# A fused attention and swish product: two more batches on tiles of the array, and an output block that opens the output product with one wait

## Chip, cores, metric

One core of one Trainium2 chip. The metric is the device time of the kernel in microseconds (us), median of several runs, with a granted TensorE clock of 0.996 to 1.0. A profiled run also has a span, which leaves out the start and the end (271.7 of 273.8 us before). Engines: PE is TensorE's matmul, DVE VectorE, ACT ScalarE, POOL GpSimd, SP SyncE.

## The reference

```python
# q, k, v: (8 batches, 8 heads, 576, 64)
q_s = softmax(q, over its 64 features);  k_s = softmax(k, over the 576 positions)
kv = einsum('bhsd,bhse->bhde', k_s, v)             # 64 x 64 a head
x  = einsum('bhsd,bhde->bhse', q_s, kv)            # to 4608 tokens x 512
h  = x @ w_in                                      # 512 -> 2048
out = (h * sigmoid(beta * h)) @ w_out              # 2048 -> 512, float32
```

## The kernel before

It works in nine slabs, t = 0 to 8: the first 512 rows of batch t, and in slab 8 the last 64 rows ("remainders") of all batches. Pass 1 of a slab computes h in 16 tiles of four 512-column matmuls; ACT empties each bank through Silu. Pass 2 is the product with w_out, from slab 1 on in a form with 7/8 of the multiplications: 112 matmuls of 256 columns on sums and differences of blocks, which DVE makes. The attention of batch t+1 is woven in (softmax, keys times values, and the outputs, which are queries times that result): `todo` holds (tick, step) pairs, a slab has 64 ticks in pass 1 and 64 in pass 2 (a product is 32/56 of a tick).

`add` records an instruction with what it reads (`r`), writes (`w`) and which PSUM banks it touches (`bank`). Waits on semaphores are derived from these; an engine that already knows of a count does not wait for it again. The eight banks are shared out:

```python
HB = (0, 1, 2)   # pass 1 tiles, in rotation; one of them takes the first product sum of pass 2
OB = (3, 4)      # the other two product sums, z5 and z2
MB = (5, 6, 7)   # attention
```

Words used below: a *block* is the output matmuls of one batch (QT with KVD), with or without remainders; a *half block* is half of them. A *key burst* is all the keys-times-values matmuls of one batch (VB with EK, and EKR for the remainder) in one go. The *transposed queries* (QT) come by a DMA transposition from slab 1 on. A *difference* is DVE's subtraction GT<-GT; the last 32 products of a pass 2 need two of them. The *entry* is what a change into tiles adds between two starts of PE. The *head* of a pass is its first few matmuls.

Batches 4 to 7 use tiles of the array: two 64-column tiles for keys times values, four 64 x 64 tiles for the output. Batches 0 to 3 multiply with full 128 x 128 matrices, one half of which is masked to zero.

```python
def tiled(b): return b > 3

def quad(b, pi=None):                   # outputs of batch b, and remainders of the pair pi
    bks = list(MB) + [HB[(hrot[0] + 1) % 3], HB[(hrot[0] + 2) % 3]]
    b_r = bks[4]                        # one bank for the remainders of both row halves
    ...                                 # x_mm, r_mm: matmuls with tile_position=(64 * a, 64 * c)
    x_mm(0, 1); r_mm(0); x_mm(0, 0); x_mm(1, 1); x_mm(1, 0); r_mm(1)
    # r_mm(1) waits on a semaphore until r_mm(0) has left the bank
    ...                                 # 4 copies to SBUF by DVE and ACT, 1 by DVE for the remainders

def attn(b):                            # slabs 4 to 6; ticks from the start of the slab
    return [(24 if b == 5 else 16, steps(kv_all, b)),
            (90, one(quad, b, b - 4 if b > 5 else None))]

def pass2_fast(t, tick, hooks):
    s, z5, z2 = HB[hrot[0] % 3], OB[0], OB[1]
    ...
    at(0)                               # ACT: exponentials of batch t + 2
    prod_s(range(0, 6)); prod(z5, ..., range(0, 6)); ...
```

The softmax here doesn't subtract the row's maximum and nothing guards it: scores larger than these inputs give would overflow.

Of the kernel before, what the change touches and what calls it, by code (L numbers as in the profile page):

```python
# [158 lines left out]
def bass_efficient_attn_shen__then__act_swish_beta_kernel(  # L159
# [12 lines left out]
    with ExitStack() as es:  # L172
# [130 lines left out]


        def tiled(b):
            return b > 3

        def pair(b, hp):
            if tiled(b):
# [133 lines left out]
        def kd(b):  # L443
            return b if b < 2 else 2 + b % 4
# [60 lines left out]
        def out_step(b, hp, pool=MB, eng=DVE):  # L505
            i = b % 2

            def one():
                bk = bank(pool)
                out_mm(b, hp, bk)  # L510
                add(eng, lambda e: (e.copy if eng == ACTE else e.tensor_copy)(  # L511
                    XT[i][:, hp, :], PS[bk][:, :]),
                    r=[("ps", bk)], w=[("xt", i, hp)], bank=[bk])
            return [one]

        def outr_steps(b):
            pi = b // 2
            st = {}

            def one(hp, e_):  # L520
                if hp == 0 and e_ == 0:
                    st["b"] = bank()
                bk = st["b"]
                c = hp * 128 + e_ * 64
                d = kd(2 * pi + e_)
                mm(PS[bk][:, c:c + 64], KVD[d][:, hp, :], QTR[:, hp, 64 * e_:64 * e_ + 64],
                   True, True, r=[("kvd", d, hp), "qtr"], w=[("ps", bk)], bk=bk)
                if hp == 3 and e_ == 1:
                    o = bass.AP(XT8, pi * 128, [[NM * SM, 128], [SM, NM], [1, 128]])
                    add(DVE, lambda e: e.tensor_copy(o, PS[bk][:, :]), r=[("ps", bk)],  # L530
                        w=[("xt8", pi)], bank=[bk])
            return [lambda hp=hp, e_=e_: one(hp, e_) for hp in range(NHP) for e_ in range(2)]

        def quad(b, pi=None):
            i = b % 2
            bks = list(MB) + [HB[(hrot[0] + 1) % 3], HB[(hrot[0] + 2) % 3]]
            b_r = bks[4]

            def x_mm(g, a):
                rows = slice(64 * a, 64 * a + 64)  # L540
                for c in range(2):
                    hp, bk = 2 * g + c, bks[2 * g + a]
                    add(PE, lambda e, c=c, hp=hp, bk=bk: e.matmul(  # L543
                        PS[bk][64 * c:64 * c + 64, :], KVD[kd(b)][rows, hp, 0:D],
                        QT[i][rows, hp, :], start=True, stop=True,
                        tile_position=(64 * a, 64 * c), skip_group_check=True),
                        r=[("kvd", kd(b), hp), ("qt", i, hp)], w=[("ps", bk)], bank=[bk])

            def r_mm(a):
                rows = slice(64 * a, 64 * a + 64)  # L550
                for g, e_, c in ([(g, e_, c) for g in range(2) for e_ in range(2)
                                  for c in range(2)] if pi is not None else ()):
                    hp, d, o = 2 * g + c, kd(2 * pi + e_), 256 * a + 128 * g + 64 * e_
                    op = add(PE, lambda e, c=c, hp=hp, d=d, o=o, e_=e_: e.matmul(
                        PS[b_r][64 * c:64 * c + 64, o:o + 64], KVD[d][rows, hp, 0:D],
                        QTR[rows, hp, 64 * e_:64 * e_ + 64], start=True, stop=True,
                        tile_position=(64 * a, 64 * c), skip_group_check=True),
                        r=[("kvd", d, hp), "qtr"], w=[("ps", b_r)], bank=[b_r])
                    if not done or done[0][0] == a:
                        done[:] = done[-1:] + [(a, op)]  # L560
                    else:
                        op.hard = [o_ for a_, o_ in done if a_ != a]

            done = []
            x_mm(0, 1)
            r_mm(0)
            x_mm(0, 0)
            x_mm(1, 1)
            x_mm(1, 0)
            r_mm(1)  # L570
            for x in (1, 0, 3, 2):
                eng, bk = (DVE, ACTE)[x % 2], bks[x]
                add(eng, lambda e, eng=eng, x=x, bk=bk: (  # L573
                    e.copy if eng == ACTE else e.tensor_copy)(XT[i][:, x, :], PS[bk][:, :]),
                    r=[("ps", bk)], w=[("xt", i, x)], bank=[bk])
            if pi is not None:
                o = bass.AP(XT8, pi * 128, [[NM * SM, 128], [SM, 2], [2 * SM, 2], [1, 128]])
                a = bass.AP(PS[b_r], 0, [[512, 128], [256, 2], [128, 2], [1, 128]])
                add(DVE, lambda e: e.tensor_copy(o, a), r=[("ps", b_r)], w=[("xt8", pi)],  # L579
                    bank=[b_r])  # L580

        def turn(b, hp0, n):
            i = b % 2
# [19 lines left out]
        def one(fn, *a):  # L603
            return lambda: fn(*a)

        def steps(fn, *a):
            return lambda: go(fn(*a))
# [2 lines left out]
            return kv_steps(b, (0, 1)) + kv_steps(b, (2, 3))  # L610

        def attn(b):
            return [(24 if b == 5 else 16, steps(kv_all, b)),
                    (90, one(quad, b, b - 4 if b > 5 else None))]

        def attn_late(b):
            if b < 4:
                x = []
                for hp in range(2):
                    x += out_step(b, hp, MB, ACTE if hp % 2 else DVE)  # L620
                s = spread(kv_steps(b, (0, 1)), 97, 101) + spread(kv_steps(b, (2, 3)), 101, 105)
                s += [(105, lambda: g_diff(1))]
                return s + spread(x, 117, 120)
            s = [(96, steps(kv_all, b)), (99, lambda: g_diff(1))]
            return s + [(112, one(quad, b))]

        def spread(steps, lo, hi):
            return [(lo + (hi - lo) * k / len(steps), s) for k, s in enumerate(steps)]
# [94 lines left out]

        def pass1_mm(t, f, m, bk):
            x = XT8 if t == 8 else XT[t % 2]
            rd = [("xt8", p_) for p_ in range(4)] if t == 8 else [("xt", t % 2, m)]
            mm(PS[bk][:, :], WIN[:, m, 128 * f:128 * f + 128], x[:, m, :], m == 0,
               m == NM - 1, r=rd + [("win", f, m)], w=[("ps", bk)], bk=bk)
            if m == NM - 1:
                add(ACTE, lambda e: e.activation(GT[:, f, :], PS[bk][:, :], ACT.Silu,  # L730
                                                 scale=BETA[:, f:f + 1]),
                    r=[("ps", bk), "beta"], w=[("gt", f, 0), ("gt", f, 1)], bank=[bk])
# [86 lines left out]
        def pass2_fast(t, tick, hooks):  # L819
# [66 lines left out]
            def at(n):  # L886
                for f in hooks.get(n, ()):
                    f()

            at(0)  # L890
            def prod_s(part):
                prod(s, lambda i, u: GS1[:, i, 128 * u:128 * u + 128], lambda i: [("gs1", i)],
# [46 lines left out]
        for t in range(NSLAB):  # L939
            todo = []  # L940
            if t == 0:
                todo = [(x, steps(t_steps, 1, (hp,), NOW, ACTE))
                        for hp, x in enumerate((97, 106, 114, 119))]
                todo += [(107, one(exp_kr_s, 1))]
                todo += [(x, one(exp_k, 1, hp, 1)) for hp, x in enumerate((108, 115, 120, 125.5))]
                todo += [(x, one(cast_v, 1, hp, DVE))
                         for hp, x in ((1, 118.5), (2, 123), (3, 127))]
                todo += [(x, steps(kv_steps, 1, (hp,), NOW))
                         for hp, x in enumerate((118, 122, 126))]
                todo += [(x, steps(out_step, 1, hp, NOW, ACTE)) for hp, x in enumerate((122.5, 125))]  # L950
                todo += [(117, one(o2_evac, 0, 0, 3, ACTE))]
                todo += [(2, steps(out_step, 0, 3, HEAD, DVE))]
            elif t < 4:
                todo = attn_late(t + 1)
                if t > 1:
                    todo += [(1, steps(out_step, t, 2, MB, ACTE)), (2.5, steps(out_step, t, 3))]
                if t == 3:
                    todo += [(4, one(norm_turn, 4, 2))]
                if t == 1:
                    todo += [(1, steps(out_step, 1, 2, (3,), ACTE)),  # L960
                             (3, steps(kv_steps, 1, (3,), (7,))),
                             (6, steps(out_step, 1, 3, (7,), DVE)),
                             (6.1, one(w_sum, 2, 4, 4)), (6.2, one(w_diff, 0)),
                             (6.3, one(w_diff, 1))]
            elif t < 7:
                todo = attn(t + 1)
                if t == 4:
                    todo += spread(outr_steps(3), 72, 88)
            elif t == 7:
                todo = spread(outr_steps(1), 32, 48)  # L970
            todo = sorted(todo, key=lambda x: -x[0])
# [151 lines left out]
```

## Time and profile before

| | before |
|---|---|
| time, median of the first 3 runs | 273.82 us |
| span of the profiled run | 271.7 us |
| PE / DVE / ACT busy | 97% / 71% / 67% |
| a slab without attention in pass 2 | 12.23 us of pass 2 |

The prediction tells how a stretch of the profile is read. In the trace of before some matmul records are missing (PE has 1918 beside 1937 weight loads); where I compare stretches, an end is put one matmul earlier if its own record is missing.

### The profile page before, as it was taken

What the parts mean: (1) busy time and instruction counts of PE and PEld (TensorE: products, weight loads), DVE (VectorE), ACT (ScalarE), POOL (GpSimd) and SP (SyncE); (2) the same over time, 40 slices, a digit from 0 to 9 for tenths busy, and PEclk for the clock granted to TensorE, in tenths of its full rate; (3) what the DMA queues carried; (4) which work ended last, traced back from release to release, by engine and by line L of the source; (5) the groups of instructions that cost most, each with busy time, mean ns of one, the idle gap of its engine ahead of it and who ended that gap; (6) DMA issues with size and microseconds to landing.
All of it is one profiled execution on the core that took longest, in us unless ns stands there. A gap on an engine that the chain in (4) does not pass through costs nothing.

```text
span 271.7 us, 4870 instructions
## 1 busy us (share of the span) xinstructions
PE 264.3 (97%) x1918; PEld 164.7 (61%) x1937; DVE 192.4 (71%) x408; ACT 181.1 (67%) x286; POOL 62.1 (23%) x80
## 2 busy tenths in 40 slices
PE   8999999999999999999999999999999999999994
PEld 2544454448844885477547864677457745874683
DVE  4964586887867799869776976678686649625762
ACT  4998658789287957897778847883783387018610
POOL 2790010006530099001900570126000100000000
PEclk9999999999999999999999999999999999999999
DMA  7999999989799139920499999112600030012005
GB/s 214 321 204 207 227 326 349 291 231 367 175 340 271 78 62 298 339 80 2 97 315 262 315 330 200 74 29 50 214 0 2 19 157 0 0 60 96 0 3 154
DMA packets 59366, 45.93 MB, mean 169 GB/s; under 512 B 28608, under 2 KB 58320, under 8 KB 58320
## 3 DMA queue, kind: packets, MB, share of 16 engines
q1 hardware_dynamic: 54480, 40.90, 53.0%
q0 software_dynamic: 4240, 4.19, 9.3%
q10 hardware_dynamic: 624, 0.53, 0.6%
q8 instruction: 15, 0.25, 0.4%
q14 instruction: 7, 0.06, 0.1%
HBM read 36.71 MB, written 9.44 MB: 170 GB/s over the span
## 4 chain that ended last, share of the span: by engine, by line
PE 88%; DVE 5%; DMA 2%; SPq 2%; issue 1%; ACT 0%
PE PS L406 51%; PE PS L830 35%; DMA VF<-in_v_dram 2%; PE PS L482 1%; PE PS L543 1%; DVE QS L357 1%; SPq L278 1%; SPq L290 1%; DVE EQ L361 1%; DVE XT L573 1%; DVE VB L377 1%; DVE TS L908 0%; DVE XT L579 0%; DVE QI L359 0%; DVE XT L511 0%
## 5 line engine op out<-in xcount | busy, mean ns | idle before, releaser
L406 PE MATMUL PS<-XT,WIN 128*128 128x512 bf16 x562 | 126.0, 379 | 1.1 <-issue 0.3
L730 ACT ACTIVATE GT<-PS,BETA 128x512 bf16<-128x512 f32 x144 | 95.2, 690 | 37.7 <-PE PS L406 37.4
L406 PEld LDWEIGHTS PS<-XT,WIN 128*128 128x128 bf16 x576 | 55.3, 98 | 64.6 <-DVE XT L511 0.6
L753 DVE TENSOR_SCALAR GT<-GT,RB 128x512 bf16<-128x512 bf16 x144 | 53.3, 392 | 36.3 <-ACT GT L730 35.5
L361 POOL TENSOR_TENSOR EQ<-EQ,QI 128x1024 bf16<-128x1024 bf16 (+1 forms) x13 | 25.6, 1967 | 50.6 <-DVE QI L359 50.0
L830 PE MATMUL PS<-WOUT,GT 128*128 128x256 bf16 x256 | 32.2, 273 | 0.4 <-DVE TS L908 0.4
L830 PE MATMUL PS<-WOUT,GS 128*128 128x256 bf16 x256 | 31.3, 273 | 0.0
L830 PE MATMUL PS<-WSUM,GT 128*128 128x256 bf16 x256 | 30.1, 273 | 0.3 <-DMA QT<-EQ 0.2
L830 PEld LDWEIGHTS PS<-WSUM,GT 128*128 128x128 bf16 x256 | 24.8, 98 | 3.9 <-issue 0.9
L830 PEld LDWEIGHTS PS<-WOUT,GT 128*128 128x128 bf16 x256 | 24.7, 98 | 3.6 <-DVE TS L908 0.9
L866 ACT COPY O2S<-PS 128x512 f32<-128x512 f32 (+1 forms) x17 | 9.4, 561 | 26.2 <-PE PS L830 25.0
L830 PEld LDWEIGHTS PS<-WOUT,GS 128*128 128x128 bf16 x256 | 24.3, 98 | 3.3 <-issue 0.4
L319 ACT ACTIVATE EQ<-QF 128x512 bf16<-128x512 f32 x32 | 18.0, 621 | 7.6 <-DMA QF<-in_q_dram 7.5
L789 DVE TENSOR_TENSOR GS<-GT 128x512 bf16<-128x512 bf16 (+2 forms) x32 | 21.9, 685 | 0.0
L357 DVE TENSOR_REDUCE QS<-EQ 128x16 f32<-128x1024 bf16 (+1 forms) x20 | 19.7, 985 | 0.8 <-ACT EQ L319 0.8
L796 DVE TENSOR_TENSOR GT<-GT 128x2048 bf16<-128x2048 bf16 x16 | 19.8, 1262 | 0.0
L377 POOL CAST VB<-VF 128x512 bf16<-128x512 f32 x24 | 14.8, 616 | 21.9 <-DVE GS L789 13.2
L319 ACT ACTIVATE EK<-KF 128x512 bf16<-128x512 f32 x32 | 18.1, 621 | 0.1
L878 DVE TENSOR_TENSOR O2S<-TS,PS 128x512 f32<-128x512 f32 (+1 forms) x17 | 10.7, 643 | 8.7 <-PE PS L830 8.7
L830 PE MATMUL PS<-WSUM,GS 128*128 128x256 bf16 x128 | 16.6, 273 | 0.0
L406 PE MATMUL PS<-WOUT,GT 128*128 128x512 bf16 x62 | 15.0, 379 | 0.1
L784 DVE TENSOR_TENSOR GS<-GT 128x256 bf16<-128x256 bf16 (+2 forms) x32 | 13.6, 426 | 1.1
(90 smaller groups left out, 215.8 us busy)
## 6 DMA issues: line engine op xcount, KB each, us to landing
out_dram<-O2S SPq DMA_DIRECT2D x8, 1024.0 KB, 5.0
QF<-in_q_dram SPq DMA_DIRECT2D x6, 1024.0 KB, 6.3
KF<-in_k_dram SPq DMA_DIRECT2D x6, 1024.0 KB, 8.7
VF<-in_v_dram SPq DMA_DIRECT2D x6, 1024.0 KB, 12.1
KF<-in_k_dram SPq DMA_DIRECT2D x8, 256.0 KB, 5.6
VF<-in_v_dram SPq DMA_DIRECT2D x8, 256.0 KB, 5.6
WOUT<-in_moe_w_out_dram POOLq DMA_DIRECT2D x4, 512.0 KB, 16.4
WIN<-in_moe_w_in_dram POOLq DMA_DIRECT2D x3, 512.0 KB, 9.2
```

The source lines that it names most:

```text
L319: add(ACTE, lambda e, o=o, a=a: e.activation(o, a, ACT.Exp), r=[(name + "f", i, hp)], w=[("e" + name, i, hp)])
L357: add(DVE, lambda e: e.tensor_reduce(s_, a, AX.X, ALU.add), r=ks, w=[("qs", i, hp0)])
L361: add(eng, lambda e: e.tensor_tensor(a, a, vb, ALU.mult), r=ks + [("qi", i, hp0)], w=ks)
L377: add(eng, lambda e: (e.copy if eng == ACTE else e.tensor_copy)(o, a), r=[("vf", i, hp), ("vone", i)], w=[("vb", i, hp)], after=after)
L406: add(PE, lambda e: e.matmul(o, l, r_, start=start, stop=stop), r=r, w=w, bank=[bk])
L730: add(ACTE, lambda e: e.activation(GT[:, f, :], PS[bk][:, :], ACT.Silu, scale=BETA[:, f:f + 1]), r=[("ps", bk), "beta"], w=[("gt", f, 0), ...
L753: add(DVE, lambda e: e.tensor_scalar(GT[:, f, :], GT[:, f, :], RB[:, f:f + 1], None, ALU.mult), r=k + ["rb"], w=k)
L784: add(DVE, lambda e: e.tensor_tensor(GS1[:, i:i + n, :], gv(i, 0, n), gv(i + NG, 1, n), ALU.add), r=gk(i, 0, n) + gk(i + NG, 1, n), w=[("g ...
L789: add(DVE, lambda e: e.tensor_tensor(GS2[:, i:i + n, :], GT[:, i:i + n, :], GT[:, i + NG:i + NG + n, :], ALU.add), r=[k_ for f in (i, i + ...
L796: add(DVE, lambda e: e.tensor_tensor(gv(f, th, NG), gv(f, th, NG), gv(f, 1 - th, NG), ALU.subtract), r=gk(f, 0, NG) + gk(f, 1, NG), w=gk(f ...
L830: add(PE, lambda e, l=l, r_=r_, st=st, u=u, i=i, b_=b_: e.matmul(PS[b_][:, 256 * u:256 * u + 256], l, r_, start=st, stop=end and i == NG - ...
L878: add(DVE, lambda e, b_=b_, u0=u0, u1=u1: e.tensor_tensor(o[:, u0:u1, :], ts[:, u0:u1, :], bank3(b_)[:, u0:u1, :], ALU.add), r=["ts", ("ps ...
```

## The change

The intent: tiles for batches 2 and 3 too, so that half of a full matmul is not spent on zeros; one wait for the whole block instead of waits inside it; two banks for the remainders, so that the two row halves run at once; and the block at the head of pass 2, so that its copies fall where DVE is idle.

```diff
-            return b > 3
+            return b > 1
@@ quad
-            bks = list(MB) + [HB[(hrot[0] + 1) % 3], HB[(hrot[0] + 2) % 3]]
-            b_r = bks[4]
+            if len(gs) == 1:
+                bks = [bank(), bank()]
+            else:
+                bks = list(MB) + [HB[(hrot[0] + 1) % 3], HB[(hrot[0] + 2) % 3], OB[1]]
+            b_r = bks[4:6]
+            first = [dict(r=..., bank=used)]        # the first tile waits for all keys and all banks
...
-            x_mm(0, 1); r_mm(0); x_mm(0, 0); x_mm(1, 1); x_mm(1, 0); r_mm(1)
+            r_mm(1); x_mm(0, 0); x_mm(0, 1); x_mm(1, 0); x_mm(1, 1); r_mm(0)
@@ attn
-            return [(24 if b == 5 else 16, steps(kv_all, b)),
-                    (90, one(quad, b, b - 4 if b > 5 else None))]
+            return [(24 if b == 5 else 16, steps(kv_all, b))]
@@ attn_late, batches 2 and 3 (slabs 1 and 2)
-            ... keys spread over ticks 97 to 105, outputs at 117 and 118.5, a DVE difference at 105
+            return [(97, steps(kv_all, b)), (97.01, lambda: g_diff(1)), (118, one(quad, b, (0,)))]
@@ pass2_fast
+            if 3 < t < 7:
+                quad(t + 1, (0, 1), t - 3)
             at(0)
@@ head of pass 1, slabs 2 and 3
-                    todo += [(1, steps(out_step, t, 2, MB, ACTE)), (2.5, steps(out_step, t, 3))]
+                    todo += [(1.5, one(quad, t, (1,)))]
@@ slab 4
-                    todo += spread(outr_steps(3), 72, 88)     # remainders of batches 2 and 3
```

(The diff is cut; statements of one kind are joined in a line.)

More of the change, by code (lines that the diff above doesn't have):

```diff
@@ L530, in one, with quad, tile @@
                     add(DVE, lambda e: e.tensor_copy(o, PS[bk][:, :]), r=[("ps", bk)],
-                        w=[("xt8", pi)], bank=[bk])
+                        w=[("xt8", pi, 0), ("xt8", pi, 1)], bank=[bk])
             return [lambda hp=hp, e_=e_: one(hp, e_) for hp in range(NHP) for e_ in range(2)]
-        def quad(b, pi=None):
+        def quad(b, gs=(0, 1), pi=None):
             i = b % 2
-            bks = list(MB) + [HB[(hrot[0] + 1) % 3], HB[(hrot[0] + 2) % 3]]
-            b_r = bks[4]
+            if len(gs) == 1:
+                bks = [bank(), bank()]
+            else:
+                bks = list(MB) + [HB[(hrot[0] + 1) % 3], HB[(hrot[0] + 2) % 3], OB[1]]
+            b_x = {2 * g + a: bks[2 * n + a] for n, g in enumerate(gs) for a in range(2)}
+            b_r = bks[4:6]
+            rem = pi is not None
+            used = list(b_x.values()) + (b_r if rem else [])
+            first = [dict(
+                r=[k_ for g in gs for c in range(2)
+                   for k_ in (("kvd", kd(b), 2 * g + c), ("qt", i, 2 * g + c))]
+                + ([("kvd", kd(2 * pi + e_), hp) for e_ in range(2) for hp in range(NHP)]
+                   + ["qtr"] if rem else []), bank=used)]
+            def tile(o, l, r_, a, c, bk, keys):
+                kw = dict(r=keys, bank=[bk])
+                if first:
+                    kw = first.pop()
+                add(PE, lambda e: e.matmul(o, l, r_, start=True, stop=True,
+                                           tile_position=(64 * a, 64 * c), skip_group_check=True),
+                    w=[("ps", bk)], **kw)
             def x_mm(g, a):
@@ L541, in x_mm @@
                 for c in range(2):
-                    hp, bk = 2 * g + c, bks[2 * g + a]
-                    add(PE, lambda e, c=c, hp=hp, bk=bk: e.matmul(
-                        PS[bk][64 * c:64 * c + 64, :], KVD[kd(b)][rows, hp, 0:D],
-                        QT[i][rows, hp, :], start=True, stop=True,
-                        tile_position=(64 * a, 64 * c), skip_group_check=True),
-                        r=[("kvd", kd(b), hp), ("qt", i, hp)], w=[("ps", bk)], bank=[bk])
-            def r_mm(a):
-                rows = slice(64 * a, 64 * a + 64)
-                for g, e_, c in ([(g, e_, c) for g in range(2) for e_ in range(2)
-                                  for c in range(2)] if pi is not None else ()):
-                    hp, d, o = 2 * g + c, kd(2 * pi + e_), 256 * a + 128 * g + 64 * e_
-                    op = add(PE, lambda e, c=c, hp=hp, d=d, o=o, e_=e_: e.matmul(
-                        PS[b_r][64 * c:64 * c + 64, o:o + 64], KVD[d][rows, hp, 0:D],
-                        QTR[rows, hp, 64 * e_:64 * e_ + 64], start=True, stop=True,
-                        tile_position=(64 * a, 64 * c), skip_group_check=True),
-                        r=[("kvd", d, hp), "qtr"], w=[("ps", b_r)], bank=[b_r])
-                    if not done or done[0][0] == a:
-                        done[:] = done[-1:] + [(a, op)]
-                    else:
-                        op.hard = [o_ for a_, o_ in done if a_ != a]
@@ L564, in quad @@
-            done = []
-            x_mm(0, 1)
-            r_mm(0)
-            x_mm(0, 0)
-            x_mm(1, 1)
-            x_mm(1, 0)
-            r_mm(1)
-            for x in (1, 0, 3, 2):
-                eng, bk = (DVE, ACTE)[x % 2], bks[x]
+                    hp, bk = 2 * g + c, b_x[2 * g + a]
+                    tile(PS[bk][64 * c:64 * c + 64, :], KVD[kd(b)][rows, hp, 0:D],
+                         QT[i][rows, hp, :], a, c, bk, [("kvd", kd(b), hp), ("qt", i, hp)])
+            def r_mm(a):
+                rows, bk = slice(64 * a, 64 * a + 64), b_r[a]
+                for g in range(2):
+                    for e_ in range(2):
+                        for c in range(2):
+                            hp, d, o = 2 * g + c, kd(2 * pi + e_), 128 * g + 64 * e_
+                            tile(PS[bk][64 * c:64 * c + 64, o:o + 64], KVD[d][rows, hp, 0:D],
+                                 QTR[rows, hp, 64 * e_:64 * e_ + 64], a, c, bk,
+                                 [("kvd", d, hp), "qtr"])
@@ new lines, in r_evac @@
+            def r_evac(a):
+                bk = b_r[a]
+                o = bass.AP(XT8, a * SM + pi * 128, [[NM * SM, 128], [2 * SM, 2], [1, 128]])
+                p = bass.AP(PS[bk], 0, [[512, 128], [128, 2], [1, 128]])
+                add(DVE, lambda e: e.tensor_copy(o, p), r=[("ps", bk)], w=[("xt8", pi, a)],
+                    bank=[bk])
+            if rem:
+                r_mm(1)
+                x_mm(0, 0)
+                x_mm(0, 1)
+                x_mm(1, 0)
+                x_mm(1, 1)
+                r_mm(0)
+                r_evac(1)
+            else:
+                for g in gs:
+                    for a in range(2):
+                        x_mm(g, a)
@@ L573, in quad @@
+            for x in sorted(b_x):
+                eng, bk = (DVE, ACTE)[x % 2], b_x[x]
                 add(eng, lambda e, eng=eng, x=x, bk=bk: (
@@ L575, in quad @@
                     r=[("ps", bk)], w=[("xt", i, x)], bank=[bk])
-            if pi is not None:
-                o = bass.AP(XT8, pi * 128, [[NM * SM, 128], [SM, 2], [2 * SM, 2], [1, 128]])
-                a = bass.AP(PS[b_r], 0, [[512, 128], [256, 2], [128, 2], [1, 128]])
-                add(DVE, lambda e: e.tensor_copy(o, a), r=[("ps", b_r)], w=[("xt8", pi)],
-                    bank=[b_r])
+            if rem:
+                r_evac(0)
         def turn(b, hp0, n):
@@ L612, in attn @@
         def attn(b):
-            return [(24 if b == 5 else 16, steps(kv_all, b)),
-                    (90, one(quad, b, b - 4 if b > 5 else None))]
+            return [(24 if b == 5 else 16, steps(kv_all, b))]
         def attn_late(b):
             if b < 4:
-                x = []
-                for hp in range(2):
-                    x += out_step(b, hp, MB, ACTE if hp % 2 else DVE)
-                s = spread(kv_steps(b, (0, 1)), 97, 101) + spread(kv_steps(b, (2, 3)), 101, 105)
-                s += [(105, lambda: g_diff(1))]
-                return s + spread(x, 117, 120)
-            s = [(96, steps(kv_all, b)), (99, lambda: g_diff(1))]
-            return s + [(112, one(quad, b))]
+                return [(97, steps(kv_all, b)), (97.01, lambda: g_diff(1)),
+                        (118, one(quad, b, (0,)))]
+            return [(96, steps(kv_all, b)), (99, lambda: g_diff(1)), (112, one(quad, b))]
         def spread(steps, lo, hi):
@@ L725, in pass1_mm @@
             x = XT8 if t == 8 else XT[t % 2]
-            rd = [("xt8", p_) for p_ in range(4)] if t == 8 else [("xt", t % 2, m)]
+            rd = [("xt8", p_, a) for p_ in range(4) for a in range(2)] if t == 8 else [("xt", t % 2, m)]
             mm(PS[bk][:, :], WIN[:, m, 128 * f:128 * f + 128], x[:, m, :], m == 0,
@@ L966, in bass_efficient_attn_shen__then__act_swish_beta_kernel @@
                 todo = attn(t + 1)
-                if t == 4:
-                    todo += spread(outr_steps(3), 72, 88)
             elif t == 7:
```

## The prediction

> **What bounds the kernel now.** I read the busy shares first, then who waits for whom on the tensor engine (PE), then the second product (from here "pass 2") slab by slab, then single instructions. From the page, and from the waits of PE, longest first (total us, times, longest):
>
> ```profile
> PE 264.3 (97%) x1918; PEld 164.7 (61%) x1937; DVE 192.4 (71%) x408; ACT 181.1 (67%) x286; POOL 62.1 (23%) x80
> ```
> ```profile
> PE PS L830 <- DVE TS L908: 0.4, 2, 0.2
> ...
> PE PS L830 <- DMA QT<-EQ: 0.2, 1, 0.2
> ...
> PE PS L406 <- ACT GT L730: 0.2, 1, 0.2
> ```
>
> After the head PE waits for almost nothing. In the trace 512-column matmuls start 216 ns apart and 256-column ones 109 ns apart, through both passes. So the time is the sum of what PE streams plus the few places where it stops, and a change is worth what it adds to or takes from that sum; DVE, ACT and DMA count only where they stop PE. Seven stretches of the same 112 products (slabs t = 1 to 7; columns: stretch, length, busy time by engine, granted clock, DMA):
>
> ```profile
> 60.66:74.68 14.02, 13.92 (x134) 12.10 (x134) 11.34 (x22) 8.55 (x15) 8.34 (x8) 1.00 0.92 275
> 88.94:102.98 14.04, 13.82 (x135) 12.13 (x134) 11.99 (x23) 10.02 (x18) 7.25 (x5) 1.00 0.32 62
> 117.29:131.04 13.75, 13.75 (x161) 11.65 (x161) 10.89 (x22) 11.84 (x22) 2.74 (x2) 1.00 0.01 2
> 145.71:158.99 13.28, 13.28 (x129) 11.36 (x128) 10.66 (x18) 10.70 (x19) 5.15 (x7) 1.00 1.10 288
> 173.66:187.33 13.67, 13.49 (x137) 11.28 (x136) 10.56 (x18) 10.29 (x18) 3.94 (x5) 1.00 0.09 21
> 202.00:215.67 13.67, 13.49 (x137) 11.26 (x137) 9.08 (x16) 6.16 (x9) 1.04 (x1) 1.00 0.00 1
> 229.71:241.94 12.23, 12.23 (x113) 10.96 (x112) 6.49 (x11) 1.89 (x4) 0.00 (x0) 1.00 0.00 1
> ```
>
> The last holds no attention work: 112 x 0.109 = 12.23. What each other slab has above 12.23 is the price of the attention put into its pass 2: 1.79, 1.81, 1.52, 1.05, 1.44, 1.44 us. That is all the change can touch, besides the few output matmuls at the head of a pass 1. Next, what tiles cost today: t = 3 (keys and outputs of batch 4), then t = 5 (outputs of batch 6 with a pair of remainders), PE alone:
>
> ```profile
> 123.60 0.32 PE L482 MATMUL PS<-VB,EK 128*64 128x65 bf16 x8
> ...
> 124.36 2.69 PE L830 MATMUL PS<-WOUT,GT 128*128 128x256 bf16 x23
> ...
> 127.52 0.63 PE L543 MATMUL PS<-QT,KVD 64*64 64x512 bf16 x8
> 128.08 0.39 PE L830 MATMUL PS<-WSUM,GT 128*128 128x256 bf16 x2
> ```
> ```profile
> 178.78 0.40 PE L543 MATMUL PS<-QT,KVD 64*64 64x512 bf16 x2
> ...
> 179.76 0.39 PE L830 MATMUL PS<-WOUT,GS 128*128 128x256 bf16 x2
> 179.99 1.91 PE L830 MATMUL PS<-WOUT,GT 128*128 128x256 bf16 x16
> 182.08 0.39 PE L830 MATMUL PS<-WOUT,GT 128*128 128x256 bf16 x2 [0.18 <-DVE TS L908]
> ```
>
> Keys of a batch: 123.60 to 124.36, 0.76. Outputs of a batch: 127.52 to 128.08, 0.56. Outputs with remainders: 178.78 to 179.76, 0.98. The product ahead of each block starts 0.20 before it instead of 0.11, so entering costs 0.09 more; the gap behind is inside the figures. At 182.08 PE stops: sixteen products take 1.75 from 179.99, to 181.74, so 0.34 is lost to DVE, which emptied the block's banks just before it was to free the bank of the next product.
>
> **The Trainium skill.** "TensorEngine Tiling (Array Packing)", section Key Properties, says that a change of tiling mode drains the engine and that tiles run independently. The trace agrees: 0.09 on entering, about 0.1 on leaving. Its Gotcha 1 says that different row tiles must not use one PSUM bank at the same time; this is why the old block has semaphores inside, and why the new one gives the remainders two banks. "TensorE: Matmul & The Clock Gate", section Measured speedup vs the span model, gives about 4 ns between starts of packed tiles; here four 512-column tiles start 3 to 4 ns apart. "ScalarE: Activation LUTs", section What ACT_TABLE_LOAD costs, gives 1283 ns for a load, as here (1.28), and another 1380 of drain, which this trace does not show: the first exponential starts 0.01 after the load.
>
> **The change, part by part.**
>
> Keys of batches 2 and 3 (t = 1, 2). Before: 20 matmuls of 131 columns, 57.5 ns each between products, 1.15. After: a block like batch 4's, 0.09 + 0.76 + 0.01 = 0.86. But in one burst they need all key exponentials at once, remainder included. At t = 1:
>
> ```profile
> 67.00 0.22 PE L406 MATMUL PS<-VB,EK 128*128 128x131 bf16 x1
> ...
> 67.71 0.23 PE L406 MATMUL PS<-VR,EKR 128*128 128x131 bf16 x1
> ```
>
> The fifth key matmul waits for the remainder's exponential, which ends at 67.65; this costs 0.16 today (1.15 + 0.16 + 0.01 = 1.32 for the batch). The burst starts at the same 67.00, reaches that matmul 0.24 later, sits until 67.71 and needs 0.61 more: out at 68.32, 1.32 in all. No gain at t = 1. At t = 2 the remainder has long been done: -0.29.
>
> Outputs of batches 2 and 3. Before: four 512-column matmuls of 0.22 per batch, two late in pass 2, two in the next pass 1. After: two half blocks. A half block is the full block less one 0.23 step: 0.56 - 0.23 + 0.09 + 0.01 = 0.43, the price of two plain matmuls (0.44). No gain but the small waits: t = 1's outputs cost 0.48 + 0.47 now, against 0.86; t = 2's 0.64 + 0.50, of which 0.16 is the wait for the transposed queries. They land when they land, so the half block still waits (I get 0.57 + 0.43 = 1.00). Together -0.09 and -0.14.
>
> Blocks of t = 4, 5, 6. They move from the middle of pass 2 to its very start. They take the remainders of batches 2 and 3 in, which at t = 4 were eight plain matmuls of 0.029 (0.23). The first tile waits for all six banks at once. The rotation of the three pass 1 banks makes two of them those of the last two pass 1 tiles. So PE stops until ACT has emptied the last tile. Around that boundary, at t = 4, ACT and PE:
>
> ```profile
> 145.71 1.47 PE L830 MATMUL PS<-WSUM,GS 128*128 128x256 bf16 x12
> 145.91 0.69 ACT L730 ACTIVATE GT<-PS,BETA 128x512 bf16<-128x512 f32 x1 [0.18 <-PE PS L406]
> 146.62 1.28 ACT L319 ACT_TABLE_LOAD   x1
> ```
>
> Today the next product starts at 145.71, before that activation has even begun: the first 24 products hide activation, scaling and sums. With the block in front, PE starts at 145.91 + 0.69 + 0.06 = 146.66: idle 0.95. The mode change is hidden in that. The block itself: per half of the rows two 512-column steps and 4 x 0.029 of remainder, in an order where one half's remainder runs beside the other's outputs: 0.56 + 0.12 = 0.68 with leaving, and I allow 0.09 for what does not overlap: 0.77. Sum 1.72 for each of the three, against 1.05, 1.44 and 1.44, which held the waits inside the block and DVE's 0.34. DVE's stop goes: it empties five pieces (about 2.1 us) while PE has 3.5 us of products ahead of DVE's next duty. ACT does its two copies ahead of the table load, so exponentials run some 1.7 us later; its next copy for PE is due about 7.0 us after the block, and I find it free with some 0.5 us to spare before PE wants the bank. So 3 x 1.72 - 3.93 = +1.23.
>
> Sum: -0.29 - 0.23 + 1.23 = +0.7 us. On 273.82: 274.5.
>
> **Rivals.**
>
> One: the wait on ACT is mostly hidden and the tiles pay. It would be so if the first tiles used banks free earlier; then 0.95 x 3 shrinks to 0.09 x 3, and the time is 273.82 + 0.7 - 2.6 = about 272. Against it: all banks are on the first tile's list, and ACT's 0.69 begins 0.42 after the last matmul's start at every boundary in the trace.
>
> Two: a follow-up wait. ACT's exponentials, 1.7 us later, delay the copy of the fourth product's bank, or DVE runs late into the bank of the third. Half a microsecond each at t = 4 and 5 makes 275.5. For it: ACT has 10.7 us of work in 13.3 at t = 4. Against it: the slack above, and DVE has its big bunch earlier.
>
> Three: the burst at t = 1 delays DVE's key scaling, and with it the difference that the last product needs. Against it: the differences before it occupy DVE until 69.95 anyway, and two scalings replace four. At most 0.3.
>
> **Range and chances.** All parts are tenths of microseconds; 2% would be 5.5 us, three times all that the three moved blocks cost. The runs of before spread over 0.5. The error is mostly the three boundaries (0.3 each way apiece, and rival two) and the key burst: 273.4 to 275.6. Within 2%: 0.97; slower 0.02; faster 0.01.
>
> **What would show it.** Pass 2 of t = 4, 5, 6 each about 13.95 long, PE idle 0.9 before the first tile with the activation of the last pass 1 tile as its releaser; no stop on DVE at t = 5 and 6; t = 1 still about 14.0 with a stop inside the key burst; t = 2 about 13.7. I am wrong if the gap at the boundary is under 0.5, if PE waits later in those passes, or if the total leaves the range because the head or the tail moved.

## The result, and the profile after

275.81 us (275.59 to 276.31, 6 runs) against 273.88 (273.44 to 274.79, 6 runs): ratio 1.0069, 95% interval 1.0052 to 1.0086. A ratio is the mean time of one kernel's fast runs over that of the other's fast runs of the same rounds, so it is not quite the ratio of the medians quoted. The change costs 0.7%. I had the direction and the class (within 2%), but said 0.7 us and it is 1.9; the time lies 0.2 us above my range.

The waits of PE in the kernel after (us in all, times, longest):

```profile
PE PS L554 <- ACT GT L744: 2.9, 3, 1.0
...
PE PS L482 <- ACT EKR L331: 0.3, 1, 0.3
PE PS L844 <- DVE GT L810: 0.3, 1, 0.3
```

The waits on DVE at line 908 of before, for the bank of the third product sum (shown in the prediction), are gone; in their place are three waits of the block (line 554) for ACT's activation, one of the key burst, and one on a DVE difference. The second products, slab by slab, as before (the three with a block begin where the last pass 1 matmul has had its 0.216):

```profile
60.75:74.92 14.17, 13.79 (x157) 11.70 (x156) 11.43 (x20) 8.54 (x15) 8.33 (x8) 1.00 0.93 269
89.20:103.22 14.02, 13.75 (x158) 11.63 (x157) 11.97 (x21) 9.99 (x18) 7.25 (x5) 1.00 0.26 53
117.66:131.41 13.75, 13.75 (x161) 11.66 (x160) 10.89 (x22) 11.93 (x23) 2.73 (x2) 1.00 0.05 10
146.09:160.17 14.08, 13.10 (x137) 11.56 (x137) 11.37 (x21) 10.80 (x19) 5.58 (x8) 1.00 1.05 289
...
231.74:243.97 12.23, 12.23 (x114) 10.97 (x113) 6.48 (x11) 1.88 (x4) 0.00 (x0) 1.00 0.01 1
```

Slabs 5 and 6 are 14.08 like slab 4. Pass 2 of slab 2, where I expected 13.66, is as long as before. Stretch by stretch (us; the before figures with missing records put right):

| stretch | before | after | difference | predicted |
|---|---|---|---|---|
| to pass 2 of slab 1 | 60.66 | 60.75 | +0.09 | 0 |
| pass 2 of slab 1 | 14.02 | 14.17 | +0.15 | -0.05 |
| pass 1 of slab 2 | 14.28 | 14.28 | 0 | -0.04 |
| pass 2 of slab 2 | 14.02 | 14.02 | 0 | -0.36 |
| pass 1 of slab 3 | 14.31 | 14.44 | +0.13 | -0.07 |
| pass 2 of slab 3 | 13.75 | 13.75 | 0 | 0 |
| slab 4, both passes | 27.95 | 28.76 | +0.81 | +0.67 |
| slab 5 | 28.34 | 28.76 | +0.42 | +0.28 |
| slab 6 | 28.34 | 28.76 | +0.42 | +0.28 |
| the rest | 56.08 | 56.07 | -0.01 | 0 |

The differences add up to 2.0, the two spans differ by 2.0. The first stretch, whose code is the same in all kernels here, takes 60.41 to 60.95 in the fifteen profiles, so its +0.09 is within what changes from run to run. The boundary of slab 4, all engines:

```profile
145.44 0.81 PE L406 MATMUL PS<-XT,WIN 128*128 128x512 bf16 x3
...
146.29 0.69 ACT L744 ACTIVATE GT<-PS,BETA 128x512 bf16<-128x512 f32 x1 [0.18 <-PE PS L406]
...
147.23 0.22 PE L554 MATMUL PS<-QTR,KVD 64*64 64x64 bf16 x3 [0.98 <-ACT GT L744]
...
147.94 0.61 PE L844 MATMUL PS<-WSUM,GS 128*128 128x256 bf16 x4
```

The activation ends at 146.97, the first tile starts at 147.23: 0.26 later, where I had allowed 0.06. In the trace, two instructions of PE's sequencer that only wait for semaphores, and then the wait of the first weight load, stand between the two. The block itself takes 0.71 (I had said 0.77). In slab 2, DVE, POOL and PE of the kernel after:

```profile
99.20 2.12 DVE L810 TENSOR_TENSOR GT<-GT 128x2048 bf16<-128x2048 bf16 x1
```
```profile
97.48 2.76 POOL L361 TENSOR_TENSOR EQ<-EQ,QI 128x1024 bf16<-128x1024 bf16 x1
```
```profile
101.47 0.38 PE L844 MATMUL PS<-WSUM,GT 128*128 128x256 bf16 x2 [0.27 <-DVE GT L810]
```

and DVE and POOL of the kernel before at the same place:

```profile
99.60 1.48 DVE L796 TENSOR_TENSOR GT<-GT 128x2048 bf16<-128x2048 bf16 x1
```
```profile
97.24 2.76 POOL L361 TENSOR_TENSOR EQ<-EQ,QI 128x1024 bf16<-128x1024 bf16 x1
```

DVE's difference starts earlier after the change, yet takes 2.12 instead of 1.48. In both kernels it ends 1.08 after the end of POOL's multiplication (101.32 and 100.24; 101.08 and 100.00). PE, some 0.4 us ahead thanks to the tiles, waits for it: its product starts 0.44 late (the 0.27 in the bracket counts only the part not covered by a modelled matmul end).

### The profile page after: what moved, and what is told of

Read it like the earlier page. It is cut to its first block, busy times and chain, and to the rows that moved or that the text cites. A ratio compares the mean times of both kernels' runs of the same rounds, so it can differ in the third digit from the quotient of the medians.

```text
span 273.8 us, 5005 instructions
## 1 busy us (share of the span) xinstructions
PE 264.2 (97%) x1993; PEld 163.5 (60%) x1993; DVE 192.1 (70%) x407; ACT 181.0 (66%) x287; POOL 62.0 (23%) x80
## 4 chain that ended last, share of the span: by engine, by line
PE 82%; DVE 7%; DMA 4%; POOL 2%; SPq 2%; issue 1%; ACT 1%; POOLq 0%; DVEq 0%
PE PS L406 49%; PE PS L844 30%; DMA VF<-in_v_dram 2%; DVE QS L357 2%; PE PS L554 1%; DMA QT<-EQ 1%; ACT GT L744 1%; DVE GT L810 1%; PE PS L482 1%; POOL VB L377 1%; SPq L290 1%; SPq L278 1%; DVE EQ L361 1%; POOL EQ L361 1%; DVE VB L377 1%
## 5 line engine op out<-in xcount | busy, mean ns | idle before, releaser
L406 PE MATMUL PS<-XT,WIN 128*128 128x512 bf16 x576 | 127.9, 379 | 0.1
L767 DVE TENSOR_SCALAR GT<-GT,RB 128x512 bf16<-128x512 bf16 x144 | 52.6, 386 | 38.9 <-ACT GT L744 38.1
L844 PE MATMUL PS<-WOUT,GS 128*128 128x256 bf16 x256 | 30.6, 273 | 0.0
L844 PE MATMUL PS<-WOUT,GT 128*128 128x256 bf16 x256 | 29.8, 273 | 0.0
L844 PEld LDWEIGHTS PS<-WOUT,GS 128*128 128x128 bf16 x256 | 25.1, 98 | 2.9
L810 DVE TENSOR_TENSOR GT<-GT 128x2048 bf16<-128x2048 bf16 x16 | 21.2, 1353 | 0.0
```

Of the source, the lines that this page charges most:

```text
L406: add(PE, lambda e: e.matmul(o, l, r_, start=start, stop=stop), r=r, w=w, bank=[bk])
L767: add(DVE, lambda e: e.tensor_scalar(GT[:, f, :], GT[:, f, :], RB[:, f:f + 1], None, ALU.mult), r=k + ["rb"], w=k)
L810: add(DVE, lambda e: e.tensor_tensor(gv(f, th, NG), gv(f, th, NG), gv(f, 1 - th, NG), ALU.subtract), r=gk(f, 0, NG) + gk(f, 1, NG), w=gk(f ...
L844: add(PE, lambda e, l=l, r_=r_, st=st, u=u, i=i, b_=b_: e.matmul(PS[b_][:, 256 * u:256 * u + 256], l, r_, start=st, stop=end and i == NG - ...
```

## The experiments

All are correct in their output, each timed in five rounds on one chip with the kernel before, whose medians in the three sets of rounds were 274.05, 274.07 and 273.89. Ratios are to it; the kernel after stands at 1.0069. Diffs are cut, and long expressions in them shortened. The start of a tile or product is compared with what the start before it allows, so a "stop" is a delay of PE's starts. The entry into tiles costs 0.09 everywhere and is not called a stop.

**1. Banks that are free.** My theory: the wait for the last activation is the cost. The rival: tiles, or the copies behind them, are slow wherever they stand.

```diff
+                if pi is not None:
+                    bks = list(MB) + [HB[hrot[0] % 3], OB[0], OB[1]]
@@ pass2_fast
+            if 3 < t < 7:
+                s, z5 = HB[(hrot[0] + 1) % 3], HB[(hrot[0] + 2) % 3]
```

> The changed kernel, but the block at the head of pass 2 of slabs 4 to 6 uses only banks that are free by then; the first two products take the banks of the last two pass 1 tiles in its stead. Theory (the wait for the activation of the last pass 1 tile is the cost): no stop ahead of the first tile, block and entry about 0.80 us instead of 1.86, each of the stretches from the head of pass 1 of slab 4, 5, 6 to the next one about 27.7 instead of 28.76, time 275.8 - 3 x 1.05 = 272.6. Rival (the tiles or the bunch of copies behind them are slow wherever they stand): 275 or more, with a stop elsewhere in those passes.

273.44 us (272.77 to 275.12), ratio 0.9985 (0.9963 to 1.0008); span 270.7. No stop ahead of the tiles; slab 4 is 27.71 long and so is slab 6. In this profile the theory holds; the median is 0.8 above the 272.6 that I expected, and 0.15% under the kernel before, which the interval does not tell from nothing. Slab 5 is 28.04: the bank lent to the second product sum is emptied late, so the third matmul of the next pass 1 waits 0.33.

```profile
159.69 0.61 PE L406 MATMUL PS<-XT,WIN 128*128 128x512 bf16 x2 [0.16 <-DVE O2S L896]
```

The runs scatter by over 2 us; the profiled one is among the fast ones, and why others are slower this experiment does not show. (The profiled run of number 11, with a like choice of banks, is one of the slow ones of its kernel: from the start of its last matmul to the end it takes 5.0 us, where the other fourteen profiles take 3.8 to 4.0. So part of the scatter can lie behind the last matmul, and not in the slabs.)

**2. One wait instead of five.** Theory: the 0.26 between activation and first tile is a row of waits worked off one by one. Rival: it is the time to wake PE.

```diff
+ if n == 12 and 3 < t < 7:      # ahead of pass 1 tile 12
+     P.pre = [writers of the block's kvd, qt and qtr]   # the next PE instruction waits for these
```

> The changed kernel, but an earlier pass 1 matmul of the same slab (first of tile 12) already waits for all that the block needs except the activations, so that the first tile of the block has one semaphore to wait for instead of five. Theory (the first tile starts 0.26 after the activation's end instead of my 0.06 because the remaining waits are worked off one after the other once the activation's semaphore has come): first tile about 0.07 after the end of the activation, time 275.8 - 3 x 0.19 = 275.2. Rival (0.26 is what it takes to wake the tensor engine on a semaphore from ACT): 275.8, unchanged.

275.17 us (274.85 to 276.06), ratio 1.0052 (1.0036 to 1.0068). ACT and PE of this kernel:

```profile
146.06 0.69 ACT L747 ACTIVATE GT<-PS,BETA 128x512 bf16<-128x512 f32 x1 [0.18 <-PE PS L409]
```
```profile
146.80 0.22 PE L557 MATMUL PS<-QTR,KVD 64*64 64x64 bf16 x2 [0.78 <-ACT GT L747]
```

The tile now starts 0.05 after the activation, and each of the three stops is 0.94 instead of 1.14. The waits that had long been satisfied cost 0.20 a block, because they stood behind the one that was late. The times agree (0.64 us won, three times 0.20 is 0.60), but the intervals of the two kernels overlap: it is the trace that shows it.

**3. The move alone**, on the kernel before (`tiled` back to `b > 3`, keys, outputs and remainders of batches 2 and 3 as before).

```diff
-            return b > 1
+            return b > 3
-                quad(t + 1, (0, 1), t - 3)
+                quad(t + 1, (0, 1), t - 3 if t > 4 else None)
@@ attn_late, head of pass 1, slab 4: the lines of the kernel before
```

> The kernel before, with only the move of the blocks to the head of pass 2 (batches 2 and 3 stay without tiles, and so do their remainders). Theory: slabs 5 and 6 lose 0.42 each; slab 4's block has no remainders, needs only the bank of the last tile but one, and stops PE about 0.2: about even with before. Time 273.9 + 0.9 = 274.8. Rival (what was not predicted comes from the tiles of batches 2 and 3 alone): the same to 0.1, but then the other half, run beside it, must account for over 1 us.

275.30 us (275.04 to 275.77), ratio 1.0052. Slabs 5 and 6 lose 0.42 each. Slab 4's block waits 0.19 for the last tile but one; the slab is 0.2 longer than before, where I said even. The profiled run also waits for the transposed queries of batch 2:

```profile
PE PS L848 <- DMA QT<-EQ: 0.9, 1, 0.9
```

The kernel before has that wait too, at most 0.03 there in its profiled run; the time at which this transposition lands differs from run to run. Without it, the span would be about 272.7, 1.0 over before: the sum of the three slabs (1.06).

**4. The tiles alone**, with the old block in the middle of pass 2.

```diff
+            return [..., (90, one(quad_old, b, b - 4))]   # quad_old: the block of the kernel before
-            if 3 < t < 7:
-                quad(t + 1, (0, 1), t - 3)
```

> The changed kernel with the old block (with its own waits inside) at its old place in the middle of pass 2; batches 2 and 3 with tiles for keys, outputs and remainders. Theory: slab 1 +0.15, pass 2 of slab 2 even (0.29 won on the keys and 0.15 on outputs, 0.44 lost to the stop on the DVE difference), head of slab 3 +0.14, slab 4 +0.38 since its block now has remainders and DVE's stop, the rest as before: 273.9 + 0.7 = 274.6. Rival (the tiles pay and only the move costs): 273.6 or less.

274.89 us (274.36 to 275.29), ratio 1.0032 (1.0019 to 1.0044). In four of its five runs 2.4 to 2.6 us lie outside the span; the span, 272.3, is only 0.5 over before. The stop on the DVE difference (0.44) and that in the head of slab 3 (0.18) are both there, and slab 4's block now has the stop on DVE that slabs 5 and 6 had (0.37). So the tiles for batches 2 and 3 do not pay here, even without the move; of the 0.5, slab 4 with its remainders in the old block has 0.43. (With the mends of numbers 6 and 7 the tiles do pay in slabs 1 to 3; see number 12.) 3 and 4 both cost; they do not add up exactly since slab 4 differs between them.

**5. The new block in the middle.**

```diff
+ (90, one(quad, b, (0, 1), b - 4))     # and not at the head of pass 2
-                bks = list(MB) + [HB[(hrot[0] + 1) % 3], HB[(hrot[0] + 2) % 3], OB[1]]
+                bks = list(MB) + [HB[(hrot[0] + 1) % 3], HB[(hrot[0] + 2) % 3], HB[hrot[0] % 3]]
```

> The changed kernel, but its new block (one wait in front, two banks for the remainders) stands in the middle of pass 2 where the old one stood, on banks that are free there. Theory (only the place costs, because of the activation): block and entry 0.80 us, then a stop of 0.3 to 0.5 on DVE, which empties five pieces (2.1 us) just before it is due to free the bank of the next product; stretches from pass 1 to pass 1 of slabs 4 to 6 about 28.0 instead of 28.76; time 275.9 - 2.2 = 273.7. Rival (the block itself, or one wait in front of all tiles, is what is slow): 275 or more.

273.84 us (273.48 to 274.06), ratio 0.9988. The waits of PE:

```profile
PE PS L844 <- DVE TS L922: 0.8, 3, 0.3
```

The block itself is no loss, one wait and all: slabs 4 to 6 take 28.13 each, against 27.95, 28.34 and 28.34 before. In the middle it costs a stop of 0.41 on DVE, at the head one of 1.14 on ACT.

**6. The copies of the second half block swapped** (first piece to ACT).

```diff
-                eng, bk = (DVE, ACTE)[x % 2], b_x[x]
+                eng, bk = (DVE, ACTE)[(x + (gs == (1,))) % 2], b_x[x]
```

> The changed kernel, with the two copies of the second half block of batches 2 and 3 swapped: the piece that pass 1 needs first goes to ACT, the other to DVE. Theory (the 0.18 stop in the head of pass 1 of slab 3 is DVE's queue, which holds a row sum and two sums ahead of that copy): the stop goes, 275.9 - 0.18 = 275.7. Rival (a half block 0.2 later than the old outputs cannot be emptied in time by any engine): the stop stays or moves to the fourth piece.

275.54 us, ratio 1.0053 (1.0035 to 1.0071). The stop of 0.18 in the head of slab 3 is gone. The time agrees, though 0.2 us is little against the spread (275.15 to 276.11).

**7. The first difference of slab 2 early.**

```diff
                 on(0, exps, 3)
+                on(0, g_diff, 0)
...
-                on(3, g_diff, 0)
```

> The changed kernel, but in slab 2 the first of the two DVE differences is issued at the start of pass 2, where DVE is idle, instead of between the row sums. Theory (DVE's differences and POOL's multiplications of the same stretch run one after the other, whichever comes first, so that the second difference ends 1.08 after POOL's second multiplication wherever it is placed): POOL's second multiplication takes about 1.9 instead of 2.76, the second difference ends about 0.9 earlier, the stop of 0.44 in pass 2 of slab 2 goes; 275.9 - 0.44 = 275.4. Rival (the second difference is late because it follows the key scaling): it stays at 2.1 us and the stop stays.

275.74 us, ratio 1.0055. DVE and POOL of slab 2:

```profile
97.51 2.49 DVE L810 TENSOR_TENSOR GT<-GT 128x2048 bf16<-128x2048 bf16 x1
```
```profile
97.01 1.91 POOL L361 TENSOR_TENSOR EQ<-EQ,QI 128x1024 bf16<-128x1024 bf16 x1
```

POOL's multiplication is back to 1.91, since no DVE difference is under way when it starts. The second difference is issued early, takes 2.49, and ends at 100.00: again 1.08 after POOL's end (98.92). The Trainium skill says this outright: "SBUF — State Buffer", section Who interferes with whom, has a DVE instruction with two SBUF inputs contend with a GpSimd instruction that reads SBUF, the later one blocked until the earlier ends. All three pairs told here agree; so does slab 1 of the kernel after, where the second difference takes 2.12 and ends 1.08 after POOL's multiplication. Where POOL is idle, the same difference takes 1.22. The stop in slab 2 is gone. But it is handed on: the head of slab 3 waits longer, for the copy that stands behind DVE's row sum.

```profile
104.49 1.04 PE L406 MATMUL PS<-XT,WIN 128*128 128x512 bf16 x4 [0.26 <-DVE XT L596]
```

**8. Key bursts later** (tick 101 for 97).

```diff
-                return [(97, steps(kv_all, b)), (97.01, lambda: g_diff(1)),
+                return [(101, steps(kv_all, b)), (101.01, lambda: g_diff(1)),
```

> The changed kernel, with the key bursts of batches 2 and 3 four ticks later (0.76 us). Theory A (the stop of 0.47 inside the burst of slab 1 is lost time): 275.9 - 0.47 = 275.4. Theory B (the transposed queries land when they land, so what is won at the burst is waited for at the half block of slab 1): the stop in the burst goes, a stop of 0.3 to 0.5 appears ahead of the half block; 275.7 to 275.9. I hold B.

275.98 us, ratio 1.0067: nothing won. The stop in the burst is gone, that on the difference in slab 2 too, and PE waits for the transposed queries instead, 0.39 and 0.43 more than the entry:

```profile
PE PS L554 <- DMA QT<-EQ: 0.7, 2, 0.4
```

In this profile theory B holds: in slab 1 the landing of the queries sets the time, not the burst.

**9. The block behind the first twelve products.** Banks, order and waits as in the change.

```diff
-            if 3 < t < 7:
-                quad(t + 1, (0, 1), t - 3)
             ...
             prod_s(range(0, 6))
+            if 3 < t < 7:
+                quad(t + 1, (0, 1), t - 3)
```

> The changed kernel, its block unchanged in banks, order and waits, but issued behind the first twelve products of pass 2 (1.31 us) instead of ahead of them. Theory (what the block pays at the head is only the activation that nothing hides): twelve products cover it, no stop ahead of the first tile, block and entry 0.80 us; stretches of slabs 4 to 6 about 27.7 instead of 28.76; 275.9 - 3.15 = 272.75. Rival (DVE, which now has its five copies nearer to the product sums, gives it back as in the middle of the pass, 0.4 each): 274.

272.50 us (272.43 to 272.89), ratio 0.9954 (0.9943 to 0.9966): 0.5% faster than the kernel before, by one moved line of the kernel after. Slab 4, both passes, of the kernel after and of this one (5 and 6 are the same to 0.01):

```profile
131.41:160.17 28.76, 27.78 (x242) 18.35 (x240) 22.39 (x47) 21.63 (x34) 10.14 (x14) 1.00 0.98 275
```
```profile
131.58:159.28 27.70, 27.70 (x242) 18.29 (x240) 22.45 (x45) 21.51 (x34) 10.71 (x13) 1.00 0.96 271
```

ACT and PE at the head of pass 2:

```profile
146.45 0.69 ACT L744 ACTIVATE GT<-PS,BETA 128x512 bf16<-128x512 f32 x1 [0.18 <-PE PS L406]
```
```profile
146.25 1.47 PE L844 MATMUL PS<-WSUM,GS 128*128 128x256 bf16 x12
147.65 0.22 PE L554 MATMUL PS<-QTR,KVD 64*64 64x64 bf16 x2
```

The activation ends at 147.14, while the twelve products run; the first tile follows them with the entry of 0.09 and nothing else. Outside the block, no start of these slabs is late by more than the 0.09 of an entry or the 0.11 of a leaving of tiles, so no stop is left, neither on ACT nor on DVE.

**10. Number 9 with 6, 7, and the first half block two ticks later.**

```diff
-                        (118, one(quad, b, (0,)))]
+                        (120, one(quad, b, (0,)))]
```

> The same, with the first difference of slab 2 early, the copies of the second half block swapped, and the first half block of batches 2 and 3 two ticks later. If the stops add up as the single runs say (0.44 in slab 2, 0.18 in the head of slab 3, up to 0.15 of waiting for the transposed queries in slab 2): 272.75 - 0.75 = 272.0, under the kernel before by 0.7%. If DVE's queue only hands the stops on, as when the difference alone was moved: 272.6 or more.

273.10 us, ratio 0.9973 (0.9960 to 0.9986): worse than 9. The half block now stands behind the start of the last product, which waits for the DVE difference (0.44 in slab 1); and the first piece is emptied too late for the head of slab 3 (0.57 with the wait):

```profile
103.66 0.60 PE L406 MATMUL PS<-XT,WIN 128*128 128x512 bf16 x2 [0.41 <-DVE XT L596]
```

**11. Free banks, another choice, with the same mends**: the last tile's bank goes to the first product sum.

```diff
+                    bks = list(MB) + [HB[hrot[0] % 3], HB[(hrot[0] + 1) % 3], OB[1]]
-            used = list(b_x.values()) + (b_r if rem else [])
+            used = list(b_x.values()) + (b_r[1:] if rem else [])
+            if 3 < t < 7:
+                s = HB[(hrot[0] + 2) % 3]
```

> The block at the head of pass 2 on banks that are free or come free within it (the bank of the last pass 1 tile is left to the first product sum), with the same three small mends. No stop ahead of the tiles, a stop of at most 0.1 ahead of the first product, which has to wait for the last activation; and no stop in the head of slab 5, where the first version of this idea lost 0.33 because DVE emptied the borrowed bank late. 272.0, as the run beside it; if the first product waits as long as the tiles did, 274.

273.65 us (273.00 to 274.77), ratio 1.0001. The first product waits 0.15, a little over what I said; slabs 4 and 5 are 27.85 and 27.86. It has the later half block of number 10 with both its stops, so the figure of 272.0 failed for the same reason, and for the 0.15.

**12. Numbers 6 and 7 together, without a moved block.**

> The changed kernel with only two mends: the first difference of slab 2 early and the copies of the second half block swapped. The early difference alone took 0.44 out of slab 2 and put 0.24 more into the head of slab 3, where the copy that pass 1 needs first stood behind DVE's row sum. Theory (that was the copy's engine): both gains stand, 275.9 - 0.44 - 0.18 = 275.3. Rival (PE, ahead of time, meets another late thing there, the transposed queries): 275.6 or more, with a stop ahead of the second half block.

275.15 us (274.63 to 275.33), ratio 1.0047 (1.0035 to 1.0059). Both stops are gone and none has come: pass 2 of slab 2 and pass 1 of slab 3 hold only the entries into tiles and a wait of 0.05 for the queries. Pass 2 of slab 1 to the end of slab 3 is now 69.87 long (69.88 in number 13), against 70.37 in the kernel before and 70.66 in the kernel after: with the two stops out of the way the tiles for batches 2 and 3 win 0.50, about what the prediction had for them (0.52).

**13. Numbers 9, 6 and 7.** The diffs of the three.

> The block behind the first twelve products, the first difference of slab 2 early, the two copies swapped; the first half block back at its tick. If the later half block is what cost the combined run its gain (its profile shows 0.57 of waiting for the first piece at the head of slab 3), the small mends stand: 272.5 - 0.44 - 0.18 = 271.9, 0.7% under the kernel before. If the mends do not add to the moved block, 272.4 or more.

272.07 us (271.63 to 272.25, 4 runs), ratio 0.9933 (0.9918 to 0.9947): the fastest here. Of the waits that the profile lists for PE, the only one after the head is the key burst of slab 1:

```profile
PE PS L482 <- ACT EKR L331: 0.3, 1, 0.3
```

## Why the prediction was right and wrong

**Right.** The mechanism of the three blocks: PE stops at each head of pass 2 until the last activation has emptied its bank, and this outweighs what the block saves. Experiment 9 moves only the place of the block, behind twelve products, and wins the 1.06 a slab that 27.70 against 28.76 shows; experiment 1 wins as much with other banks, but for the 0.33 that these lose in slab 5. DVE's old stop is gone. ACT, with its exponentials 1.9 us later, stays in time, so the second rival did not come. The burst of slab 1 gains nothing, and the moved half blocks cost what two matmuls cost (0.44 against 0.43, the wait for queries apart). The 0.52 for slabs 1 to 3 is there too, but only in experiments 12 and 13; in the kernel after two stops eat it.

**Wrong, 1: the term "145.91 + 0.69 + 0.06 = 146.66: idle 0.95".** The 0.06 came from a wait of PE in before, at 182.08, whose weight load has a single wait in the trace. Here 0.26 passes; experiment 2 shows that 0.20 of it is the other waits of that first tile (it gathers those for keys and queries beside "all six banks at once"), worked off after the late one. I saw in the diff that all needs were gathered in one instruction, and priced it as one wait. With the block 0.06 shorter than said, that is 0.14 a slab, 0.42 in all.

**Wrong, 2: the third rival, "at most 0.3" and put down to slab 1.** I reasoned that DVE is busy until 69.95 anyway and that fewer scalings bring the second difference forward. They do, but its end hangs on POOL's multiplication. In before it ended just before PE wanted it (101.08, and the product starts at 101.23); with the keys 0.29 quicker, PE comes too early, and the -0.36 for slab 2 becomes 0. That DVE's subtraction takes 1.48 there in before, and 1.22 where POOL is idle, was in the trace and told of it; I did not read it.

**Wrong, 3: the heads of pass 1, priced by PE alone.** For slab 3 I had -0.07 and it is +0.13, because the piece needed first went from ACT to DVE, where a row sum of the next batch stands ahead (experiment 6).

**Smaller.** In slab 1 the half block waits 0.15 for the transposed queries, which I had put only into slab 2; when they land differs from run to run (0 to 0.9 in the profiles here). The 0.09 ahead of pass 2 of slab 1 is no more than the scatter between profiles. Two statements of the prediction are wrong and changed nothing: DVE empties four pieces of a block and not five (147.94 to 149.88 in slab 4; ACT has two), and 5.5 us is not three times what the three blocks cost but about as much (3 x 1.72 = 5.16).

These terms are 0.42, 0.36, 0.20, 0.24 (pass 2 of slab 1 and the pass 1 behind it) and 0.09: 1.31, which is the 1.3 us between the sum of 0.7 and the 2.0 of the profile. The range was too narrow for the number of places where PE now arrives earlier at something that comes at its own time.

## What to carry to other kernels

When one instruction gathers all the waits of a block, it takes the latest of them for every tile, and the waits standing behind that one are paid on top (0.20 here); put such a block where the latest need is already met (here twelve products later), or let an earlier instruction take up the others. Where the bound engine gets faster, ask at each next meeting point what the other side hangs on: a DMA's landing or a chain of DVE and POOL kept its time here, and the gain turns into a wait. One copy in the wrong engine's queue can hold what a tile has saved.

## What the Trainium skill lacked or had wrong

- "TensorEngine Tiling (Array Packing)", Key Properties, says that a change of mode drains the engine, but not what it costs: here 0.09 us on entering and about 0.1 on leaving, between streams of matmuls.
- "Perfetto Trace Analysis", Identifying Dependency Chains, says that an instruction that waits for several engines may have EventSemaphore instructions put ahead of it. It does not say that they are worked off in order, so that those behind the late one add time even when long satisfied: 0.20 us for two such instructions and a third wait (0.26 against 0.05 after the release).
- "ScalarE: Activation LUTs", What ACT_TABLE_LOAD costs, has 1380 ns of drain beside the load; here the load of 1.28 starts 0.02 us after the activation ahead of it ends, and the exponential 0.01 after the load, so no such drain is visible.
- On "SBUF — State Buffer", Who interferes with whom, nothing was wrong: the difference ended 1.08 us after POOL's multiplication in every pair told, with the difference taking 1.48 to 2.49 us.
